# The off-diagonal parts of a block-diagonal product formed in one pass, and another order of the first loads, in a linear-attention and MLP kernel

## Chip, cores and metric

The kernel runs on one core of a Trainium2 chip. The metric is the device time of one execution in microseconds (us). Engines are named as in the profile: PE (TensorE, products), PEld (its weight loads), DVE (VectorE), ACT (ScalarE), POOL (GpSimd), SP (SyncE, which issues most DMAs). ACT has a DMA queue of its own. Each profiled span is shorter than the time of its execution, and not by the same amount everywhere: by 2.0 to 2.3 us in the kernels with the old overhang code, by about 1.7 us (1.7 to 2.0) in those with the new one.

## The reference, cut to what matters

```python
x = A_x                                  # [1, 2048, 640]
xn = _layernorm(x)
qkv = xn @ wqkv                          # 32 heads of 20 columns
pq, pk = phi(q), phi(k)                  # phi(t) = where(t > 0, t + 1, exp(t)) + 1e-6
kv  = einsum("bhsd,bhse->bhde", pk, v)   # one 20x20 matrix per head
num = einsum("bhqd,bhde->bhqe", pq, kv)
den = einsum("bhqd,bhd->bhq", pq, z) + 1e-6
out = x + (num / den) @ wo + mlp(xn)     # mlp: 640 -> 1536 -> 640, gelu
```

The kernel never forms v. It forms G = xnᵀ·pk and then kv = wvᵀ·G, masked to the heads, and KVW = kvᵀ·wo, so that attention ends in a single product with pq.

Of the kernel before, what the change touches and what calls it, by code (L numbers as in the profile page):

```python
# [9 lines left out]
ALU = mybir.AluOpType  # L10
BF16 = mybir.dt.bfloat16
# [4 lines left out]
def kernel(  # L16
# [12 lines left out]
    nc = tc.nc  # L29
    P = nc.NUM_PARTITIONS  # L30
# [3 lines left out]
    S, D = x2d.shape  # L34
    F = B_w1.shape[1]
    H = 32
    DH = D // H
    NT = S // P
    NC = D // P
    NJ = F // P  # L40
    TOK = 512
    NG = S // TOK
    TPG = TOK // P
    EPS = 1e-5
    HALF = D // 2
# [1 line left out]
    assert S % TOK == 0 and D % P == 0 and F % P == 0 and D == H * DH  # L47
    assert REST * TPG == TOK and NG * H == P

    e_lo = [m * P // DH * DH for m in range(NC)]  # L50
    e_rest = [min(H, (m * P + P - 1) // DH + 1) * DH - e_lo[m] - P for m in range(NC)]
    SKEW = DH - 4
    assert all(0 < r <= H for r in e_rest) and all(m * P - e_lo[m] <= SKEW for m in range(NC))

    ctx.enter_context(nc.allow_non_contiguous_dma(reason="small strided setup transfers"))

    consts = ctx.enter_context(tc.tile_pool(name="consts", bufs=1))
# [12 lines left out]
    GT = persist.tile([P, NC, D], BF16, name="GT")  # L70
    zacc = persist.tile([P, D], F32, name="zacc")
# [4 lines left out]
    wqk = early.tile([P, NC, 2 * D], BF16, name="wqk", tag="early")  # L76
    pk = mid.tile([P, NT, D], BF16, name="pk", tag="mid")

    wv = consts.tile([P, NC, D], BF16, name="wv")
    w1 = consts.tile([P, NC, F], BF16, name="w1")  # L80
    woA = consts.tile([P, NC, D], BF16, name="woA")
# [19 lines left out]
    def bank(dtype=F32, hold=False):  # L101
        n = turn.pop(0)
        if isinstance(hold, str):
            named[hold] = n
        else:
            (held if hold else turn).append(n)
        return psum.tile([P, TOK if dtype == F32 else 2 * TOK], dtype, name=f"bank{n}", tag=f"bank{n}")
# [16 lines left out]
    def load_x(t0, t1, queue=nc.sync):  # L124
        queue.dma_start(out=x_all[:, t0:t1, :], in_=xv[:, t0:t1, :])

    def load_wk(k0, k1):
        nc.scalar.dma_start(out=wqk[:, k0:k1, D : 2 * D], in_=wqkv_v[:, k0:k1, D : 2 * D])

    load_x(0, 1)  # L130
    load_x(1, 2, nc.scalar)
    load_x(2, 3)
    load_x(3, 4)

# [8 lines left out]

    nc.vector.memset(eps_t[:], EPS)
    nc.vector.memset(neg_half[:], -0.5)
    load_wk(0, 3)
    load_wk(3, NC)
    load_x(4, 8, nc.scalar)
# [13 lines left out]
            )  # L162

    WIDE = SKEW + P + H
    emask = consts.tile([P, NC + 2, WIDE], mybir.dt.int8, name="emask")
    emask_u = emask[:, :, SKEW : SKEW + P]

    def emask_parts():
        def select(block, q, base, sign, shift):
            nc.gpsimd.affine_select(  # L170
                out=emask[q, block, SKEW - shift : SKEW - shift + H // 4 * DH],
                in_=emask[q, block, SKEW - shift : SKEW - shift + H // 4 * DH],
                compare_op=ALU.is_ge, fill=0.0, base=base,
                pattern=[[-sign * DH, H // 4], [0, DH]], channel_multiplier=sign,
            )

        parts = [lambda: nc.gpsimd.memset(emask[:], 1.0)]
        for m in range(NC):
            i = m % NG
            for block, q, first in ((m, slice(0, P), 0), (NC + m // NG, slice(i * H, (i + 1) * H), P)):  # L180
                for base, sign in ((first, 1), (DH - 1 - first, -1)):
                    parts.append(
                        lambda block=block, q=q, base=base, sign=sign, m=m: select(block, q, base, sign, m * P - e_lo[m])
                    )
        return parts

    def emit_warm(n):
# [74 lines left out]
    def fill(it, n=None):  # L262
        for emit in it[:n]:
            emit()
        del it[:n]
# [94 lines left out]
    def gate(ap):  # L360
        nc.gpsimd.tensor_copy(out=gate_t[:], in_=ap)
# [93 lines left out]
    def emit_G_sums(*names):  # L455
        for name in names:
            out, a, b = {
                "S1": lambda: (g_S(1), g_S(2), g_left(0, 0)),
                "S2": lambda: (g_S(2), g_left(1, 1), g_S(3)),
                "S3": lambda: (g_S(3), g_left(0, 0), g_left(1, 0)),  # L460
                "S4": lambda: (g_S(4), g_left(0, 1), g_S(2)),
                "T1": lambda: (g_T(1), by_deep(g_right(0, 1)), by_deep(g_right(0, 0))),
                "T2": lambda: (g_T(2), by_deep(g_right(1, 1)), g_T(1)),
                "T3": lambda: (g_T(3), g_right(1, 1), g_right(0, 1)),
                "T4": lambda: (by_deep(g_T(4)), by_deep(g_right(1, 0)), g_T(2)),
            }[name]()
            nc.vector.tensor_tensor(out=out, in0=a, in1=b, op=ALU.add if name == "S1" else ALU.subtract)
# [274 lines left out]
    quads = [Quad(m) for m in range(NR)]  # L742
    q = quads[0]
# [21 lines left out]
    for q, last, (w, den) in zip(quads[1:], quads, work):  # L765
        q.P5()
        last.close("b" if last.m else "c")
        last.P7_odd()
        q.P6()
        fill(w, 0 if den else None)  # L770
        if last.m:
            last.close("c")
        last.close("f", gelu=False)
        fill(w)
        if q.m + 1 < NR and not den:
            quads[q.m + 1].P1()
        q.P7()
        last.gelu("f")
        if den:
            fill(den)  # L780
            quads[q.m + 1].P1()
    gate(hT[NG - 1][:, 2, 0:1])
    fill(emask_work)
    last = quads[-1]
# [95 lines left out]
    def scale(g, c, part=slice(0, TOK)):  # L880
        gs = slice(g * TOK + part.start, g * TOK + part.stop)
        nc.vector.tensor_tensor(out=pqT[:, c, gs], in0=pqT[:, c, gs], in1=xnT[:, c, gs], op=ALU.mult)  # L882
# [9 lines left out]
    load_rec(0)  # L892
    for m in range(NC):
        nc.sync.dma_start(out=woA[:, m, :], in_=A_wo[e_lo[m] : e_lo[m] + P, :])
    woB = zacc[:].bitcast(BF16).rearrange("p (a n) -> p a n", a=2)
    for m in range(NC):
        a, i = divmod(m, NG)
        r = e_rest[m]
        nc.sync.dma_start(
            out=woB[i * H : i * H + r, a, :], in_=A_wo[e_lo[m] + P : e_lo[m] + P + r, :]  # L900
        )
    emit_G_sums("T1", "T2", "T3", "S1")
    for t in (1, 1 + NH):
        emit_xb(t)
# [12 lines left out]
    first, second = (  # L917
        [lambda c=c, g=g, p=p: scale(g, c, p) for g in (2, 0) for c in range(NC)]
        for p in (slice(0, 2 * P), slice(2 * P, TOK))
    )  # L920
# [4 lines left out]
        both(lambda b: (b.product(name, p), b.done(name, k, r, c), fill(rest, ns[b.i])))  # L925

    late = mid.tile([P, NT, D], BF16, name="late", tag="mid")
    kv = late[:, 0:2, :].rearrange("p a n -> p (a n)")[:, 0 : (NC + 2) * P].rearrange("p (b n) -> p b n", n=P)
    KVW = late[:, 2 : 2 + NC, :]
    osbs = [late[:, 2 + NC + i, :] for i in range(6)]  # L930
    Tq = wv[:].rearrange("p c n -> p (c n)")[:, 0 : 4 * CH * HALF].bitcast(FP16).rearrange(
# [90 lines left out]
    kvps = [bank(), bank()]  # L1022
    for m in range(NC):
        a, i = divmod(m, NG)
        for j in range(NC):
            nc.tensor.matmul(
                kvps[a][:, i * P : (i + 1) * P], lhsT=wv[:, j, e_lo[m] : e_lo[m] + P],
                rhs=GT[:, j, m * P : (m + 1) * P], start=(j == 0), stop=(j == NC - 1),
            )
    for a in range(2):  # L1030
        ms = range(a * NG, min(NC, (a + 1) * NG))
        for j in range(NC):
            for m in ms:
                i = m % NG
                r = min(H, D - e_lo[m] - P)
                nc.tensor.matmul(
                    kvps[1][i * H : i * H + r, (a + 1) * P : (a + 2) * P],
                    lhsT=wv[:, j, e_lo[m] + P : e_lo[m] + P + r],
                    rhs=GT[:, j, m * P : (m + 1) * P], start=(j == 0), stop=(j == NC - 1),
                )  # L1040
    fill(rest)
    ps0 = kvps[0][:].rearrange("p (b n) -> p b n", n=P)
    ps1 = kvps[1][:].rearrange("p (b n) -> p b n", n=P)
    nc.vector.tensor_tensor(out=kv[:, 0:NG, :], in0=ps0, in1=emask_u[:, 0:NG, :], op=ALU.mult)
    nc.vector.tensor_tensor(
        out=kv[:, NG : NG + 2, :], in0=ps1[:, 0:2, :], in1=emask_u[:, NG : NG + 2, :], op=ALU.mult
    )
    r = e_rest[NC - 1]
    nc.vector.tensor_tensor(
        out=kv[0:r, NG + 2, :], in0=ps1[0:r, 2, :], in1=emask_u[0:r, NG + 2, :], op=ALU.mult  # L1050
    )

    def emit_KVW(ns):
        pss = [bank() for _ in range(NC)]
        for m, ps in enumerate(pss):
            nc.tensor.matmul(ps[:, 0:HALF], lhsT=kv[:, m, :], rhs=woA[:, m, ns], start=True, stop=False)
        for m, ps in enumerate(pss):
            a, i = divmod(m, NG)
            q = slice(i * H, i * H + e_rest[m])
            nc.tensor.matmul(  # L1060
                ps[:, 0:HALF], lhsT=kv[q, NC + a, :], rhs=woB[q, a, ns], start=False, stop=True
            )
        for m, ps in enumerate(pss):
            (nc.vector.tensor_copy if m % 2 and ns is halves[0] else nc.scalar.copy)(out=KVW[:, m, ns], in_=ps[:, 0:HALF])  # L1064

    p = pairs[0]
    p.open("b", hold=True)
    p.h("b", 2, True)
    emit_KVW(halves[0])
    fill(S_sums(0, q_of, Sq_of))  # L1070
    p.open("f", hold=True)
# [31 lines left out]
    for n, p in enumerate(pairs):  # L1103
        first, last = n == 0, n == NH - 1
        late = late_scales[: LATE[n]]
# [122 lines left out]
```

## The kernel before: the parts that the change touches

Loads at the start. `x_all` holds 16 tiles of 128 tokens (160 KB each). Tiles 0 to 3 are the first group, and are worked on one by one; tiles 4 to 7 come as one DMA with rows of 5 KB instead of 1.25 KB.

```python
load_x(0, 1)                    # SP queue
load_x(1, 2, nc.scalar)         # ACT queue
load_x(2, 3)                    # SP
load_x(3, 4)                    # SP
...
load_wk(0, 3)                   # K weights, ACT, 480 KB
load_wk(3, NC)                  # K weights, ACT, 320 KB
load_x(4, 8, nc.scalar)         # ACT, 640 KB
```

After this comes, for each tile: mean and variance on DVE (two halves), norm on DVE, transpose on PE, and the K product on PE. DVE takes these steps in program order (see the lines below), so it stops at the first tile that has not come.

kv near the end. D = 640 is five blocks of 128 columns, and a head has 20 columns, so each block of kv has an overhang of up to 32 rows beside its 128x128 diagonal part:

```python
for m in range(NC):                               # five diagonal blocks
    for j in range(NC):                           # 25 products 128x128x128
        nc.tensor.matmul(kvps[a][...], lhsT=wv[:, j, e_lo[m] : e_lo[m] + P], rhs=GT[:, j, m * P : (m + 1) * P], ...)
for a in range(2):                                # overhangs
    ...                                           # 25 products with 12 or 32 stationary columns
            nc.tensor.matmul(kvps[1][i * H : i * H + r, (a + 1) * P : (a + 2) * P],
                lhsT=wv[:, j, e_lo[m] + P : e_lo[m] + P + r], rhs=GT[:, j, m * P : (m + 1) * P], ...)
# DVE: three masked copies into kv; then for each half of the columns:
for m, ps in enumerate(pss):
    nc.tensor.matmul(ps[:, 0:HALF], lhsT=kv[:, m, :], rhs=woA[:, m, ns], start=True, stop=False)
for m, ps in enumerate(pss):                      # overhang, K = 12 to 32 rows, 128 columns
    nc.tensor.matmul(ps[:, 0:HALF], lhsT=kv[q, NC + a, :], rhs=woB[q, a, ns], start=False, stop=True)
```

## Time and profile before

| | before |
|---|---|
| median time | 197.51 us (6 runs, 197.21 to 199.71) |
| profiled execution | 200.89 us, span 198.7 us, mean granted clock 0.99 |
| PE in the chain that ended last | 93% |

The first lines are from the page of the kernel before: the span, PE's busy time, and the heads of the chain of waits followed back from the last instruction.

```profile
span 198.7 us, 3380 instructions
PE 191.3 (96%) x1260; PEld 112.3 (57%) x1260; DVE 163.3 (82%) x392; ACT 89.8 (45%) x165; POOL 21.1 (11%) x52
...
PE 93%; DMA 4%; DVE 1%; SPq 0%; issue 0%
```

PE bounds the kernel; apart from it only a wait for an x tile at the start shows. The next lines are the timeline of that start: start in us, duration in us, engine, line, operation, out<-in, count, and in brackets the idle time before it and what ended it.

```profile
0.80 0.39 ACTq L125 DMA_DIRECT2D x_all<-in_A_x_dram  x1
0.81 1.42 SPq L125 DMA_DIRECT2D x_all<-in_A_x_dram  x3
...
1.22 1.00 ACTq L128 DMA_DIRECT2D wqk<-in_A_wqkv_dram  x2
...
2.25 0.49 ACTq L125 DMA_DIRECT2D x_all<-in_A_x_dram  x1
...
4.04 0.89 DVE L201 BATCH_NORM_STATS2 stats<-x_all 128x6 f32<-128x320 bf16 x2 [3.07 <-DMA x_all<-in_A_x_dram]
...
9.75 0.49 DVE L201 BATCH_NORM_STATS2 stats<-x_all 128x6 f32<-128x320 bf16 x1 [1.75 <-DMA x_all<-in_A_x_dram]
10.16 0.43 DVE L221 TENSOR_SCALAR xn<-x_all,mv,rstd 128x640 bf16<-128x640 bf16 x1
...
10.65 0.71 PE L234 MATMUL bank_197<-identity,xn 128*128 128x128 bf16 x5 [1.86 <-DVE xn L221]
```

DVE waits for tile 0 until 4.04 us and for tile 3 until 9.75 us. The norm of tile 2 stands behind the statistics of tile 3 in program order, so it starts at 10.16 and PE at 10.65. This profile is of a slow run. Now the kv stage, same view and columns:

```profile
126.52 1.28 PE L1026 MATMUL bank_1440<-GT,wv 128*128 128x128 bf16 x20
...
127.64 0.44 PE L1026 MATMUL bank_1441<-GT,wv 128*128 128x128 bf16 x5
...
128.01 0.73 PE L1036 MATMUL bank_1441<-GT,wv 128*32 128x128 bf16 x25
...
128.67 0.99 PE L964 MATMUL bank_1498<-w_93,hT_79 128*128 128x320 bf16 x6
...
130.28 0.30 PE L1060 MATMUL bank_1508<-zacc,late 12*128 12x320 bf16 x1
130.42 0.29 PE L1060 MATMUL bank_1509<-zacc,late 12*128 12x320 bf16 x1
130.64 0.66 PEld L964 LDWEIGHTS <-xn 128*128 128x128 f16 x6 [0.26 <-issue]
130.65 0.99 PE L964 MATMUL bank_1529<-w_91,xn 128*128 128x320 f16 x6
```

L1036 is the 25 overhang products: 0.66 us from their start to that of the next product. L1060 is the overhang of KVW: its fifth product starts 0.14 us behind the fourth.

### The profile page before, as it was taken

The numbers are of one execution on the slowest core, as the hardware profiler recorded it, in microseconds if no ns is written. First come the engines' busy times: TensorE is split into PE (matmuls) and PEld (weight loads), VectorE is DVE, ScalarE is ACT, GpSimd is POOL, SyncE is SP. The second block draws the span as 40 slices with busy tenths as digits, with TensorE's granted clock in tenths as the row PEclk, the third lists the DMA queues.
The fourth block names the chain that finished last, engine by engine and source line by source line (L and its number), as shares of the span: only waits on it lengthen the run. The fifth ranks groups of instructions, "written<-read, shape, count | busy, mean of one in ns | idle before, by whom it ended". The sixth has DMA issues, their size and how long they took to land.

```text
span 198.7 us, 3380 instructions
## 1 busy us (share of the span) xinstructions
PE 191.3 (96%) x1260; PEld 112.3 (57%) x1260; DVE 163.3 (82%) x392; ACT 89.8 (45%) x165; POOL 21.1 (11%) x52
## 2 busy tenths in 40 slices
PE   7589999999999999999999999999999999999993
PEld 2255444544445454444444777757777777777772
DVE  1659896999699999879688889979999999786533
ACT  2427767457669768899786320050010010100100
POOL 1001244002308500000700000000000000000000
PEclk9969999999999999999999999999999999999999
DMA  5999524964134100000006975400200110110113
GB/s 199 335 290 380 183 61 107 311 223 93 39 132 106 30 0 2 0 0 3 0 0 145 335 235 164 139 0 2 69 0 0 69 66 13 55 69 0 66 35 101
DMA packets 24400, 20.15 MB, mean 101 GB/s; under 512 B 11120, under 2 KB 24000, under 8 KB 24384
## 3 DMA queue, kind: packets, MB, share of 16 engines
q1 hardware_dynamic: 23280, 18.13, 29.7%
q10 hardware_dynamic: 1104, 1.80, 2.5%
q8 instruction: 10, 0.16, 0.4%
q14 instruction: 6, 0.05, 0.1%
HBM read 12.72 MB, written 5.24 MB: 90 GB/s over the span
## 4 chain that ended last, share of the span: by engine, by line
PE 93%; DMA 4%; DVE 1%; SPq 0%; issue 0%
DMA x_all<-in_A_x_dram 4%; PE bank_1209 L795 2%; PE bank_1282 L824 2%; PE bank_1273 L824 2%; PE bank_2131 L964 1%; PE bank_2047 L964 1%; PE bank_1963 L964 1%; PE bank_1879 L964 1%; PE bank_1790 L964 1%; PE bank_1701 L964 1%; PE bank_1575 L964 1%; PE bank_1433 L964 1%; PE bank_1398 L824 1%; PE bank_1386 L824 1%; PE bank_205 L310 1%; PE bank_1529 L964 1%
## 5 line engine op out<-in xcount | busy, mean ns | idle before, releaser
L964 PEld LDWEIGHTS <-xn 128*128 128x128 f16 x198 | 19.0, 98 | 7.3 <-issue 0.3
L485 PEld LDWEIGHTS <-w_91 128*128 128x128 bf16 x120 | 11.7, 98 | 13.9
L201 DVE BATCH_NORM_STATS2 stats<-x_all 128x6 f32<-128x320 bf16 x32 | 13.7, 469 | 4.8 <-DMA x_all<-in_A_x_dram 4.8
L473 PEld LDWEIGHTS <-wqk 128*128 128x128 bf16 x100 | 9.6, 98 | 11.1
L310 PEld LDWEIGHTS <-xnT 128*128 128x128 bf16 x80 | 7.6, 103 | 7.2 <-issue 0.7
L824 PEld LDWEIGHTS <-xn 128*128 128x128 bf16 (+1 forms) x80 | 7.8, 98 | 3.0
L221 DVE TENSOR_SCALAR xn<-x_all,mv,rstd 128x640 bf16<-128x640 bf16 x16 | 6.2, 436 | 3.6 <-POOL rstd L217 3.6
L882 DVE TENSOR_TENSOR pqT<-pqT,xnT 128x256 bf16<-128x256 bf16 (+1 forms) x30 | 8.5, 326 | 0.0
L320 PEld LDWEIGHTS <-xnT 128*128 128x128 bf16 x80 | 6.0, 101 | 3.9 <-issue 0.6
L628 PEld LDWEIGHTS <-w_91 128*128 128x128 bf16 (+1 forms) x48 | 4.5, 98 | 5.8 <-issue 0.7
L979 PEld LDWEIGHTS <-Sq 128*128 128x128 f16 x66 | 6.4, 98 | 2.4
L170 POOL TENSOR_SCALAR_AFFINE_SELECT emask<-emask 128x160 int8<-128x160 int8 (+1 forms) x20 | 7.1, 362 | 1.2
L412 DVE TENSOR_TENSOR x_all<-x_all,b2b 128x640 bf16<-128x640 bf16 x16 | 7.0, 479 | 0.0
L271 DVE TENSOR_SCALAR pqT<-pqT 128x512 bf16<-128x512 bf16 x20 | 5.7, 284 | 0.7 <-ACT pqT L268 0.6
L979 PEld LDWEIGHTS <-pqT 128*128 128x128 bf16 x50 | 4.8, 98 | 1.9 <-issue 0.3
L964 PEld LDWEIGHTS <-hT_79 128*128 128x128 bf16 x48 | 4.6, 98 | 1.9
L964 PEld LDWEIGHTS <-hT_80 128*128 128x128 bf16 x48 | 4.7, 98 | 1.7
L1064 ACT CAST late<-bank_1505 128x320 bf16<-128x320 f32 x1 | 0.4, 426 | 10.9 <-PE bank_1509 L1060 10.9
L190 PE MATMUL bank_124<-const-bfloat16-1.0 128*128 128x512 bf16 x10 | 3.7, 546 | 0.8 <-PEq L1212 0.8
L873 DVE TENSOR_TENSOR Sq<-pqT 128x256 f16<-128x256 bf16 x16 | 4.3, 281 | 0.0
L727 DVE TENSOR_TENSOR pk<-pk,GT 128x512 bf16<-128x512 bf16 x10 | 4.2, 421 | 0.0
L628 PEld LDWEIGHTS <-wv 128*128 128x128 f16 x24 | 2.3, 98 | 3.0 <-issue 0.3
(645 smaller groups left out, 510.7 us busy)
## 6 DMA issues: line engine op xcount, KB each, us to landing
xnT<-rec_rows SPq DMA_DIRECT2D x20, 128.0 KB, 2.5
out_dram<-late SPq DMA_DIRECT2D x14, 160.0 KB, 1.9
w_91<-in_B_w_dram SPq DMA_DIRECT2D x2, 960.0 KB, 6.6
w_93<-in_B_w_dram SPq DMA_DIRECT2D x3, 640.0 KB, 7.6
x_all<-in_A_x_dram SPq DMA_DIRECT2D x2, 640.0 KB
wqk<-in_A_wqkv_dram SPq DMA_DIRECT2D x1, 800.0 KB, 7.9
wv<-in_A_wqkv_dram SPq DMA_DIRECT2D x1, 800.0 KB
woA<-in_A_wo_dram SPq DMA_DIRECT2D x5, 160.0 KB, 3.1
```

The source lines that it names most:

```text
L170: nc.gpsimd.affine_select(out=emask[q, block, SKEW - shift : SKEW - shift + H // 4 * DH], in_=emask[q, block, SKEW - shift : SKEW - shift ...
L201: nc.vector.bn_stats(out=st[:, half, :], in_=x_all[:, t, half * HALF : (half + 1) * HALF])
L221: nc.vector.tensor_scalar(out=xn[:, t, ds], in0=x_all[:, t, ds], scalar1=mv[:, t, 0:1], scalar2=rstd[:, t : t + 1], op0=ALU.subtract, op1= ...
L310: nc.tensor.matmul(K_ps[t][:], lhsT=xnT[:, k, t * P : (t + 1) * P], rhs=wqk[:, k, D : D + TOK], start=(k == 0), stop=(k == NC - 1),)
L412: nc.vector.tensor_tensor(out=x_all[:, t, :], in0=x_all[:, t, :], in1=b2b[:], op=ALU.add)
L473: nc.tensor.matmul(ps[:], lhsT=wqk[:, k, m * P : (m + 1) * P], rhs=xnT[:, k, gs], start=(k == 0), stop=(k == NC - 1),)
L485: nc.tensor.matmul(ps[:], lhsT=w1[:, k, j * P : (j + 1) * P], rhs=xnT[:, k, g * TOK : (g + 1) * TOK], start=(k == 0), stop=(k == NC - 1),)
L628: nc.tensor.matmul(self.ps[name][:], lhsT=left[:, c, js], rhs=x_block(*block, c) if block else Tx({4: 3, 5: 0, 6: 1, 7: 2}[p], c), start=( ...
L824: nc.tensor.matmul(ps if len(right.shape) == 3 else ps.rearrange("p (c n) -> p c n", c=NC), lhsT=left[:, t, self.i], rhs=right[:, t], star ...
L882: nc.vector.tensor_tensor(out=pqT[:, c, gs], in0=pqT[:, c, gs], in1=xnT[:, c, gs], op=ALU.mult)
L964: nc.tensor.matmul(self.ps[name][:, cols], lhsT=left[:, j], rhs=right[:, j, cols], start=(start and j == 0), stop=False, skip_group_check= ...
L979: nc.tensor.matmul(self.ps[name][:, cols], lhsT=left[:, c], rhs=right[:, c, cols], start=False, stop=(stop and c == CH - 1), skip_group_ch ...
```

## The change

It has three parts. The overhangs: instead of 25 products, five of full size give four windows of 32x32, which cover four of the overhangs (the last block is moved so that it ends with the matrix, which makes its overhang an 8-column piece of the fourth). The loads: x tile 1 goes to SP, and the K weights wait for a memset on their target. The order: the product P1 of the next MLP step is put ahead of the attention denominators. Cut to its core:

```diff
-    load_x(1, 2, nc.scalar)
+    load_x(1, 2)
...
+    nc.vector.memset(wqk[:, 0, D : D + TOK], 0.0)
     load_wk(0, 3)
...
         if den:
+            quads[q.m + 1].P1()
             fill(den)
-            quads[q.m + 1].P1()
...
+    nc.gpsimd.tensor_copy(out=wvw..., in_=wv[:, :, P : P + NG * WE]...[:, :, :, 0:H])   # the four windows' columns
...
-    for a in range(2):           # 25 products on strips
-        ...
+    wins = kvps[1][:, P : 2 * P].rearrange("p (i n) -> p i n", i=NG)
+    for j in range(NC):
+        nc.tensor.matmul(wins, lhsT=wvw[:, j], rhs=GT[:, j, P - H + 8 : ...][:, :, 0:H], start=(j == 0), stop=(j == NC - 1))
...
-            nc.tensor.matmul(ps[:, 0:HALF], lhsT=kv[q, NC + a, :], rhs=woB[q, a, ns], start=False, stop=True)
+            nc.tensor.matmul(ps[rows, 0:HALF], lhsT=kvw[q, i, cols], rhs=woB[q, ns], start=False, stop=True, ...)
```

Here `rows` and `cols` pick a 32x32 square (8 columns for the fifth), so that a product uses 32 rows and 32 columns of the PE array.

More of the change, by code (lines that the diff above doesn't have):

```diff
@@ L48 @@
     assert REST * TPG == TOK and NG * H == P
-    e_lo = [m * P // DH * DH for m in range(NC)]
-    e_rest = [min(H, (m * P + P - 1) // DH + 1) * DH - e_lo[m] - P for m in range(NC)]
+    e_lo = [m * P // DH * DH for m in range(NC - 1)] + [D - P]
+    WQ, WE = P - 24, P - 8
     SKEW = DH - 4
-    assert all(0 < r <= H for r in e_rest) and all(m * P - e_lo[m] <= SKEW for m in range(NC))
+    assert DH == 20 and NC == 5 and all(m * P % DH <= SKEW for m in range(NC))
     ctx.enter_context(nc.allow_non_contiguous_dma(reason="small strided setup transfers"))
@@ L164, with select, heads @@
     WIDE = SKEW + P + H
-    emask = consts.tile([P, NC + 2, WIDE], mybir.dt.int8, name="emask")
+    emask = consts.tile([P, NC + 1, WIDE], mybir.dt.int8, name="emask")
     emask_u = emask[:, :, SKEW : SKEW + P]
     def emask_parts():
-        def select(block, q, base, sign, shift):
+        def select(out, base, sign, pattern):
             nc.gpsimd.affine_select(
-                out=emask[q, block, SKEW - shift : SKEW - shift + H // 4 * DH],
-                in_=emask[q, block, SKEW - shift : SKEW - shift + H // 4 * DH],
-                compare_op=ALU.is_ge, fill=0.0, base=base,
-                pattern=[[-sign * DH, H // 4], [0, DH]], channel_multiplier=sign,
+                out=out, in_=out, compare_op=ALU.is_ge, fill=0.0, base=base, pattern=pattern, channel_multiplier=sign
+            )
+        def heads(block, q, e0, q0, sign):
+            start = q0 - q0 % DH
+            select(
+                emask[q, block, SKEW - q0 % DH :][:, 0 : H // 4 * DH], e0 - start if sign > 0 else start + DH - 1 - e0,
+                sign, [[-sign * DH, H // 4], [0, DH]],
             )
         parts = [lambda: nc.gpsimd.memset(emask[:], 1.0)]
-        for m in range(NC):
-            i = m % NG
-            for block, q, first in ((m, slice(0, P), 0), (NC + m // NG, slice(i * H, (i + 1) * H), P)):
-                for base, sign in ((first, 1), (DH - 1 - first, -1)):
-                    parts.append(
-                        lambda block=block, q=q, base=base, sign=sign, m=m: select(block, q, base, sign, m * P - e_lo[m])
-                    )
+        areas = [(m, slice(0, P), e_lo[m], m * P) for m in range(NC)]
+        areas += [(NC, slice(i * H, (i + 1) * H), P + i * WE, WQ + i * P) for i in range(NG)]
+        for area in areas:
+            for sign in (1, -1):
+                parts.append(lambda area=area, sign=sign: heads(*area, sign))
+        w3 = emask[3 * H :, NC, SKEW:]
+        e3 = P + 3 * WE
+        parts.append(lambda: select(w3[:, 0 : P - WQ], e3 - e_lo[3] - P, 1, [[0, P - WQ]]))
+        parts.append(lambda: select(w3[:, P - WQ : H], e_lo[4] - 1 - e3, -1, [[0, H - (P - WQ)]]))
         return parts
@@ L894 @@
         nc.sync.dma_start(out=woA[:, m, :], in_=A_wo[e_lo[m] : e_lo[m] + P, :])
-    woB = zacc[:].bitcast(BF16).rearrange("p (a n) -> p a n", a=2)
-    for m in range(NC):
-        a, i = divmod(m, NG)
-        r = e_rest[m]
-        nc.sync.dma_start(
-            out=woB[i * H : i * H + r, a, :], in_=A_wo[e_lo[m] + P : e_lo[m] + P + r, :]
-        )
+    woB = zacc[:].bitcast(BF16)[:, 0:D]
+    for i in range(NG):
+        nc.sync.dma_start(out=woB[i * H : (i + 1) * H, :], in_=A_wo[P + i * WE : P + i * WE + H, :])
+    wvw = zacc[:].bitcast(BF16)[:, D : 2 * D].rearrange("p (c n) -> p c n", c=NC)
+    nc.gpsimd.tensor_copy(
+        out=wvw.rearrange("p c (i n) -> p c i n", i=NG),
+        in_=wv[:, :, P : P + NG * WE].rearrange("p c (i n) -> p c i n", i=NG)[:, :, :, 0:H],
+    )
     emit_G_sums("T1", "T2", "T3", "S1")
@@ L927 @@
     late = mid.tile([P, NT, D], BF16, name="late", tag="mid")
-    kv = late[:, 0:2, :].rearrange("p a n -> p (a n)")[:, 0 : (NC + 2) * P].rearrange("p (b n) -> p b n", n=P)
+    kv = late[:, 0, :].rearrange("p (b n) -> p b n", n=P)
+    kvw = late[:, 1, 0 : NG * (H + 8)].rearrange("p (i n) -> p i n", i=NG)
+    nc.gpsimd.memset(kvw[:, :, 0:8], 0.0)
     KVW = late[:, 2 : 2 + NC, :]
@@ L1029 @@
             )
-    for a in range(2):
-        ms = range(a * NG, min(NC, (a + 1) * NG))
-        for j in range(NC):
-            for m in ms:
-                i = m % NG
-                r = min(H, D - e_lo[m] - P)
-                nc.tensor.matmul(
-                    kvps[1][i * H : i * H + r, (a + 1) * P : (a + 2) * P],
-                    lhsT=wv[:, j, e_lo[m] + P : e_lo[m] + P + r],
-                    rhs=GT[:, j, m * P : (m + 1) * P], start=(j == 0), stop=(j == NC - 1),
-                )
+    wins = kvps[1][:, P : 2 * P].rearrange("p (i n) -> p i n", i=NG)
+    for j in range(NC):
+        nc.tensor.matmul(
+            wins, lhsT=wvw[:, j],
+            rhs=GT[:, j, P - H + 8 : P - H + 8 + NG * P].rearrange("p (i n) -> p i n", i=NG)[:, :, 0:H],
+            start=(j == 0), stop=(j == NC - 1),
+        )
     fill(rest)
     ps0 = kvps[0][:].rearrange("p (b n) -> p b n", n=P)
-    ps1 = kvps[1][:].rearrange("p (b n) -> p b n", n=P)
     nc.vector.tensor_tensor(out=kv[:, 0:NG, :], in0=ps0, in1=emask_u[:, 0:NG, :], op=ALU.mult)
+    nc.vector.tensor_tensor(out=kv[:, NG, :], in0=kvps[1][:, 0:P], in1=emask_u[:, NG, :], op=ALU.mult)
     nc.vector.tensor_tensor(
-        out=kv[:, NG : NG + 2, :], in0=ps1[:, 0:2, :], in1=emask_u[:, NG : NG + 2, :], op=ALU.mult
-    )
-    r = e_rest[NC - 1]
-    nc.vector.tensor_tensor(
-        out=kv[0:r, NG + 2, :], in0=ps1[0:r, 2, :], in1=emask_u[0:r, NG + 2, :], op=ALU.mult
+        out=kvw[:, :, 8:], in0=wins, in1=emask_u[:, NC, 0:H].unsqueeze(1).to_broadcast((P, NG, H)), op=ALU.mult
     )
@@ L1055, in emit_KVW @@
         for m, ps in enumerate(pss):
-            nc.tensor.matmul(ps[:, 0:HALF], lhsT=kv[:, m, :], rhs=woA[:, m, ns], start=True, stop=False)
+            nc.tensor.matmul(ps[:, 0:HALF], lhsT=kv[:, m, :], rhs=woA[:, m, ns], start=True, stop=True)
         for m, ps in enumerate(pss):
-            a, i = divmod(m, NG)
-            q = slice(i * H, i * H + e_rest[m])
+            i, rows, cols = (m, slice(P - H, P), slice(0, H)) if m < NG else (NG - 1, slice(0, 8), slice(H, H + 8))
+            q = slice(i * H, (i + 1) * H)
             nc.tensor.matmul(
-                ps[:, 0:HALF], lhsT=kv[q, NC + a, :], rhs=woB[q, a, ns], start=False, stop=True
+                ps[rows, 0:HALF], lhsT=kvw[q, i, cols], rhs=woB[q, ns], start=False, stop=True, skip_group_check=True
             )
```

## The prediction

> **What bounds the kernel now.** TensorE. In the chain of work that ended last, PE is 93% of the 198.7 us span. From 10.65 us on the chain stays on PE; before that it is one DMA (x_all, 4%) and VectorE. The profiled run was slow (200.89 us against a median of 197.51).
>
> **The start.** In the timeline VectorE's first statistics wait for x tile 0 until 4.04 us; then VectorE is nearly gapless (stats 0.9, center 0.4, stats 0.9 ...) until it waits for x tile 3, which landed at 9.75 us. That holds norm(2) until 10.16 and PE until 10.65, and the granted clock falls to 0.5 until 13.6 us. About 2 us of wait and 1.5 us of clock: just the 3.4 us by which this run is slow. The DMA packets show x tile 3 done by about 6.5 us on nearly all engines; on one its rows alternated with the 5 KB rows of tiles 4 to 7 until 9.2. I take it that the fast runs don't have this wait and are bound by tile 0's landing and VectorE. The Trainium skill ("DMA: Bandwidth & Descriptors", "Queues, rings and completion order") says each DMA engine round-robins between the queue rows; the alternating packets agree.
>
> The change sends tile 0 first and alone: tile 1 moves behind it on SP, and the K weights wait for a VectorE memset (estimate 0.2 to 0.3 us, from the 0.28 us of a 128x512 bf16 tensor_scalar). Both tiles' packets now share 1.9 to 3.5 us, so tile 0 should land 0.3 to 0.5 us earlier, and PE's start with it: **-0.4 us**. Against it: x tile 3 is now the fourth issue on SP, nearer to x tiles 4 to 7, and may land later (needed by about 7.7 us).
>
> **P1 before the denominators.** PE waits about 0.15 us for Z3t (0.32 us on VectorE) before the 20 den products at 95.01. P1 (0.43) fits there: **-0.1 us**.
>
> **kv.** The 25 strip products take 128.01 to 128.67: 26 ns each, 0.66 us, plus a gap of about 0.08. Five 128x128x128 products at 56 ns (as the 20 before them) are 0.28: **-0.4 us**. VectorE's masking stays about equal (0.68+0.42+0.27 against 0.68 and two of 0.27). It starts at 128.19 because VectorE is busy until then; the first K=128 product of KVW needs the 128x512 part, about 128.9, and PE will be there at about 129.1. So the saving is just not swallowed.
>
> **KVW rests.** From 130.18 to 130.65 per half: four K=12..32 products start together at 130.28, the fifth 0.14 later. With 32x32 squares the four still overlap; the fifth shares their row group but not their columns, so it may overlap: 0 to -0.14 per half, **-0.1 us** in all.
>
> Off the path: the POOL copy of wv's columns (estimate 1 to 1.5 us near 116).
>
> Sum: about -1.1 us. **Predicted 196.4 us, range 195.4 to 197.6.** Faster by over 2%: 0.05; within 2%: 0.93; slower: 0.02.
>
> **What would show it.** First statistics at about 3.6 us; kv plus rests on PE about 1.4 us, not 1.98; no wait between P7 and den; KVW's first product with no wait for the mask.
>
> **What would make it wrong.** x tile 3 later or earlier than I think: if the fast runs did have the 9.75 us wait and the new order cures it, -3 us; if tile 3 slips past 8 us, +1 to +3. POOL's copy slowing VectorE before 128 us.

## The result

| | before | after |
|---|---|---|
| median | 197.40 us (20 runs, 197.01 to 199.71) | 197.26 us (10 runs, 196.95 to 197.46) |
| ratio of fast runs | | 0.998, 95% interval 0.9958 to 1.0002 |
| profiled | 198.7 us span (slow) | 195.3 us span (fast) |

A ratio here is the mean time of one kernel's fast runs over that of the other's in the same rounds, so it is not quite the ratio of the medians that are quoted. The verdict is "same": a gain of 0.4 us by the ratio, of 0.14 by the medians, and none is inside the interval, where 1.1 us were forecast. The time lies in the forecast range, the gain does not come near its forecast size.

The start after the change, same view as before:

```profile
0.81 1.82 SPq L125 DMA_DIRECT2D x_all<-in_A_x_dram  x4
...
0.99 0.27 DVE L146 MEMSET wqk<- 128x256 uint32 x1
...
1.29 0.96 ACTq L128 DMA_DIRECT2D wqk<-in_A_wqkv_dram  x2
...
2.28 0.49 ACTq L125 DMA_DIRECT2D x_all<-in_A_x_dram  x1
...
3.06 0.89 DVE L209 BATCH_NORM_STATS2 stats<-x_all 128x6 f32<-128x320 bf16 x2 [1.80 <-DMA x_all<-in_A_x_dram]
...
6.13 0.89 DVE L209 BATCH_NORM_STATS2 stats<-x_all 128x6 f32<-128x320 bf16 x2 [0.46 <-DMA x_all<-in_A_x_dram]
...
8.66 0.49 DVE L209 BATCH_NORM_STATS2 stats<-x_all 128x6 f32<-128x320 bf16 x1 [1.09 <-DMA x_all<-in_A_x_dram]
9.07 0.43 DVE L229 TENSOR_SCALAR xn<-x_all,mv,rstd 128x640 bf16<-128x640 bf16 x1
...
13.12 1.24 PE L318 MATMUL bank_255<-wqk,xnT 128*128 128x512 bf16 x5
```

Tile 0 comes 1 us earlier (3.06). But DVE now waits 0.46 us for tile 2 and 1.09 us for tile 3, and the norm of tile 2 starts at 9.07. The last line is the last K product of the first group; the chain of waits has been on PE since 9.55 us. Against the kernel before, the gate moves next to nothing: the K weights are issued at 1.29 instead of 1.22, because before the change the ACT queue was busy with x tile 1 until then. But with tile 1 off that queue they would go out at 0.80 without a gate, and that is worse (`no_gate` below).

The kv stage after the change:

```profile
123.72 1.28 PE L1037 MATMUL bank_1442<-GT,wv 128*128 128x128 bf16 x20
...
125.12 0.44 PE L1043 MATMUL bank_1443<-GT,zacc 128*128 128x128 bf16 x5
...
125.40 0.98 PE L975 MATMUL bank_1480<-w_93,hT_79 128*128 128x320 bf16 x6
...
127.00 0.30 PE L1063 MATMUL bank_1490<-zacc,late 32*32 32x320 bf16 x1
127.00 0.29 PE L1063 MATMUL bank_1491<-zacc,late 32*8 32x320 bf16 x1
127.23 0.66 PEld L975 LDWEIGHTS <-xn 128*128 128x128 f16 x6
127.23 0.99 PE L975 MATMUL bank_1511<-w_91,xn 128*128 128x320 f16 x6
```

From the start of the diagonal products to the next MLP product it is now 125.40 - 123.72 = 1.68 us (2.15 before), and the fifth overhang product of KVW starts with the fourth. So the kv part did what was hoped, and more.

### The profile page after: what moved, and what is told of

Read it like the earlier page. It is cut to its first block, busy times and chain, and to the rows that moved or that the text cites. A ratio compares the mean times of both kernels' runs of the same rounds, so it can differ in the third digit from the quotient of the medians.

```text
span 195.3 us, 3345 instructions
## 1 busy us (share of the span) xinstructions
PE 189.1 (97%) x1240; PEld 111.4 (57%) x1240; DVE 163.7 (84%) x393; ACT 89.8 (46%) x165; POOL 22.3 (11%) x54
## 4 chain that ended last, share of the span: by engine, by line
PE 93%; DMA 3%; DVE 1%; SPq 1%; issue 0%
DMA x_all<-in_A_x_dram 3%; PE bank_1210 L803 2%; PE bank_1283 L832 2%; PE bank_1274 L832 2%; PE bank_2113 L975 1%; PE bank_2029 L975 1%; PE bank_1945 L975 1%; PE bank_1861 L975 1%; PE bank_1772 L975 1%; PE bank_1683 L975 1%; PE bank_1557 L975 1%; PE bank_1435 L975 1%; PE bank_1399 L832 1%; PE bank_1387 L832 1%; PE bank_1511 L975 1%; PE bank_2042 L975 1%
## 5 line engine op out<-in xcount | busy, mean ns | idle before, releaser
L318 PEld LDWEIGHTS <-xnT 128*128 128x128 bf16 x80 | 7.3, 98 | 7.5 <-issue 0.9
L328 PEld LDWEIGHTS <-xnT 128*128 128x128 bf16 x80 | 5.8, 98 | 3.5
L172 POOL TENSOR_SCALAR_AFFINE_SELECT emask<-emask 128x160 int8<-128x160 int8 (+3 forms) x20 | 6.7, 347 | 0.9
```

What stands on the lines that cost most here:

```text
L172: nc.gpsimd.affine_select(out=out, in_=out, compare_op=ALU.is_ge, fill=0.0, base=base, pattern=pattern, channel_multiplier=sign)
L318: nc.tensor.matmul(K_ps[t][:], lhsT=xnT[:, k, t * P : (t + 1) * P], rhs=wqk[:, k, D : D + TOK], start=(k == 0), stop=(k == NC - 1),)
```

## Experiments

**A fast profile of the kernel before.** The first profile was slow, so it could not be set against the one after. The unchanged kernel was profiled again.

> The kernel before, unchanged, for a profile in the fast state (the one at hand is slow by 3.4 us). Theory A (the new load order delays x tile 3 and eats what kv gains): a fast run has no wait for x tile 3, or a short one; tile 3 is usable by about 8.2 us; PE's last K tile starts near 12.5 us (13.28 after the change); and from there to the end it takes 182.7 us as in the slow profile (182.0 after the change). Theory B (the start is as good as before or better, and the kv part saved nothing in the fast state): the last K tile starts at 13.3 us or later and the rest takes about 182.0 us. Theory C: the slow state is not the start at all; then the start looks as in the slow profile, with tile 3 at 9.75 us and the clock at 0.5.

It came out at 197.42 us, span 195.2 us, clock 1.0. The timeline of its start:

```profile
4.04 0.89 DVE L201 BATCH_NORM_STATS2 stats<-x_all 128x6 f32<-128x320 bf16 x2 [3.07 <-DMA x_all<-in_A_x_dram]
...
7.90 0.49 DVE L201 BATCH_NORM_STATS2 stats<-x_all 128x6 f32<-128x320 bf16 x1
...
8.30 0.43 DVE L221 TENSOR_SCALAR xn<-x_all,mv,rstd 128x640 bf16<-128x640 bf16 x1
...
12.35 1.24 PE L310 MATMUL bank<-wqk,xnT 128*128 128x512 bf16 x5
```

After tile 0 nothing is waited for. The norm of tile 2 starts at 8.30 us, against 9.07 after the change (+0.77), and the last K product at 12.35 against 13.12 (+0.77). Theory A stands: the start has become 0.77 us slower. The extra time of the slow profile is the wait for tile 3 (norm of tile 2 at 10.16 instead of 8.30) and the lower clock behind it (a mean of 0.57 from 10 to 14 us, and 1.0 here), since the two profiles differ in nothing else of that size. Other slow runs were not profiled. That the wait brought the clock down is not shown: in the profile of `no_gate` below PE waits longer (2.25 us, until 9.74), and the clock stays at 1.0.

**The two halves of the change alone.** `loads_only` is the kernel before with the two load edits; `rest_only` is the change without them.

```diff
 loads_only, on the kernel before:
-    load_x(1, 2, nc.scalar)
+    load_x(1, 2)
+    nc.vector.memset(wqk[:, 0, D : D + TOK], 0.0)
 rest_only, on the changed kernel: the same three lines the other way round
```

> Before, with the change's load order alone (x tile 1 on SP, memset ahead of the K weights). Theory A: 0.5 to 0.9 us slower than before; tile 3 statistics again start near 8.7 us with a wait of about 1 us on the DMA. Theory B: same as before or up to 0.4 us faster. My prediction said 0.4 us faster.

> The change without its load order (x tile 1 back on the ACT queue, no memset); kv, KVW and P1 parts kept. Theory A: 0.5 to 0.8 us faster than before, so about 196.7 us. Theory B: no faster than 0.2 us. The prediction's sum for these parts was 0.6.

`loads_only`: 198.50 us median, ratio to before 1.0053 (1.0036 to 1.0070), so about 1.0 us slower. `rest_only`: 196.40 us, ratio 0.9953 (0.9933 to 0.9973), so about 0.9 us faster. The two nearly cancel, as the result says. The rival, that kv saved nothing, falls. The start of `loads_only`, and then PE's last product in the fast profiles of the kernel before, the change, `rest_only` and `loads_only`, in this order:

```profile
6.33 0.89 DVE L202 BATCH_NORM_STATS2 stats<-x_all 128x6 f32<-128x320 bf16 x2 [0.63 <-DMA x_all<-in_A_x_dram]
...
8.44 0.49 DVE L202 BATCH_NORM_STATS2 stats<-x_all 128x6 f32<-128x320 bf16 x1 [0.67 <-DMA x_all<-in_A_x_dram]
...
12.90 1.24 PE L311 MATMUL bank<-wqk,xnT 128*128 128x512 bf16 x5
```

```profile
191.91 0.22 PE L986 MATMUL bank<-late,pqT 128*128 128x128 bf16 x1
191.84 0.22 PE L997 MATMUL bank_2134<-late,pqT 128*128 128x128 bf16 x1
191.04 0.22 PE L996 MATMUL bank<-late,pqT 128*128 128x128 bf16 x1
192.46 0.22 PE L987 MATMUL bank<-late,pqT 128*128 128x128 bf16 x1
```

In `loads_only` tiles 2 and 3 are waited for as after the change, tile 3 for less than the 1 us expected, and the last K product starts 0.55 us late (12.90 against 12.35). PE ends 0.87 us earlier in `rest_only`, in line with its time, and 0.55 us later in `loads_only`: the rest of its 1.0 us lies behind PE's last product or outside the span, and is not explained.

**What delays tiles 2 and 3.** `x4_sp` takes x tiles 4 to 7 from the ACT queue and puts them behind tile 3 on SP.

```diff
     load_x(3, 4)
+    load_x(4, 8)
...
-    load_x(4, 8, nc.scalar)
```

> The whole change, with x tiles 4 to 7 moved from the ACT queue to the SP queue, behind x tile 3, so that tile 3 shares the DMA engines with the K weights alone. Theory A: tile 3 lands by about 7.5 us, no wait for it, PE's last K tile starts about 1.2 us earlier than after the change (near 12 us), and the time is 0.8 to 1.3 us below the change, near 196.2. Rival A2 (it is the later K weights, which made PE wait until 6.29 us for its first K product, not tile 3): less than 0.3 us gained, since the K weights come no earlier here.

196.03 us median, ratio 0.9932 (0.9913 to 0.9951): the fastest of all, 0.7% below before. Theory A's time came out, but not by its path, and rival A2 falls on the time. The profiled run (196.65 us, the slowest of its six) shows:

```profile
6.92 0.89 DVE L209 BATCH_NORM_STATS2 stats<-x_all 128x6 f32<-128x320 bf16 x2 [1.13 <-DMA x_all<-in_A_x_dram]
...
8.05 0.59 PE L318 MATMUL bank<-wqk,xnT 128*128 128x512 bf16 x2 [0.83 <-DMA wqk<-in_A_wqkv_dram]
```

Tile 3 isn't waited for any more; tile 2 and the second K weights are. The last K product starts at 12.73 us, 0.4 us earlier than after the change, and this run is 0.4 us faster than the profiled run of the change. What the faster runs of this kernel look like was not profiled.

**How long the K weights are held back.** Three kernels differ from the change in one line each: no memset at all, one of 888 words, one of 1280.

```diff
 no_gate:    -    nc.vector.memset(wqk[:, 0, D : D + TOK], 0.0)
 gate_mid:   -    nc.vector.memset(wqk[:, 0, D : D + TOK], 0.0)
             +    nc.vector.memset(wqk[:, 0:3, D : D + TOK + 80], 0.0)
 gate_long:  -    nc.vector.memset(wqk[:, 0, D : D + TOK], 0.0)
             +    nc.vector.memset(wqk[:, 0:4, D : D + TOK + P], 0.0)
```

> The whole change without its memset; x tile 1 stays on SP, so the K weights are the first issue of the ACT queue at 0.80 us. Theory F: the first K weights (480 KB) go ahead of x tile 1, whose statistics wait beyond 5 us; x tiles 2 and 3 come later still, behind x tiles 4 to 7; time 0.5 to 2 us above the change. Rival R: within 0.3 us of the change, since 0.3 us of gate more or less does little.

> The whole change with a longer memset ahead of the K weights (888 instead of 256 words a partition, estimate 0.93 us from the 0.27 us of the change's), so that they are issued near 1.95 us: after x tile 2 (1.7) and before x tile 3 (2.2). Theory F (the data moves about in the order in which the two queues issue, so it matters before which x tile the K weights are issued): tile 2 follows tile 1 at once and lands by 4.8 us; no wait for it; tile 3 still comes late, usable near 7 us; norm of tile 2 near 7.6 to 8.3 us; time 0.5 to 1.2 us below the change. Rival R (the queues share the DMA engines row by row from the start, so a gate only shifts the K weights by its own length): tile 2 gains at most 0.3 us, tile 3 is still waited for past 8.3 us, time within 0.3 us of the change.

> The whole change with a memset of 1280 words (estimate 1.33 us), so that the K weights are issued near 2.36 us, after all four x tiles. Theory F: tiles 0 to 3 land one after the other, tile 3 by about 5 us; VectorE never waits for a tile after tile 0; the K weights land near 6 and 7 us, so that the first K products wait instead; norm of tile 2 near 7.6 us, last K tile near 11.9 us (13.28 after the change), time 0.8 to 1.4 us below the change, near 196.1. Rival R: as for the mid gate, within 0.3 us of the change.

On where the tiles go, theory F was right. These are KB moved by the two queues in half microseconds, added up from the DMA packets of the traces by the time at which each ended (SP / ACT; up to 7.5 us SP carries x tiles 0 to 3, without tile 1 in the kernel before):

| us | before, fast | after | gate_long |
|---|---|---|---|
| 2.0 to 3.0 | 82 / 105 | 203 / 0 | 264 / 0 |
| 3.0 to 4.0 | 123 / 214 | 109 / 123 | 241 / 0 |
| 4.0 to 4.5 | 89 / 105 | 1 / 179 | 54 / 14 |
| 4.5 to 5.5 | 54 / 328 | 152 / 224 | 75 / 243 |
| 5.5 to 6.5 | 127 / 224 | 80 / 287 | 0 / 344 |
| 6.5 to 7.5 | 6 / 390 | 72 / 308 | 0 / 346 |

After the change tile 2, third on SP (its issue starts near 1.7 us), has to let the first K weights (issued at 1.29) go ahead: from 4.0 to 4.5 us SP moves 1 KB. Tile 3 then meets tiles 4 to 7. With the long gate all four tiles are through by about 5 us. In these traces the order of issue over both queues decides about when a DMA starts to move. It does not decide the shares from then on: there the rows of the two queues take turns, which favours the 5 KB rows of tiles 4 to 7.

The medians were `gate_mid` 198.68 us (ratio 1.0056), `gate_long` 198.13 (1.0022), `no_gate` 198.06 (1.0060). For `no_gate` this is what F expected, 0.8 us above the change; for the two gates it is not. Their runs fall into two kinds. Of the long gate's six, two took 196.55 and 196.71 us at clock 1.0 (0.6 us below the change), three 198.5 to 198.9 at 0.988 to 0.990, and one 197.74 at 1.0. Of the mid gate's six, one took 196.77 and one 198.04 us at 1.0, and four 198.3 to 199.7 at 0.989 or 0.990. All of them count as fast. The quick ones come near F: in the profile of `gate_mid` (196.77 us) tile 2 is not waited for and its norm starts at 8.12, but PE waits 1.00 and 0.42 us for K weights. The profile of a quick run of `gate_long` shows what is waited for there:

```profile
2.36 0.97 ACTq L128 DMA_DIRECT2D wqk<-in_A_wqkv_dram  x2
...
7.16 1.44 PE L318 MATMUL bank<-wqk,xnT 128*128 128x512 bf16 x5 [1.55 <-DMA wqk<-in_A_wqkv_dram]
7.36 0.43 DVE L229 TENSOR_SCALAR xn<-x_all,mv,rstd 128x640 bf16<-128x640 bf16 x1
```

The norm of tile 2 starts at 7.36 us, 1.7 us earlier than after the change, but PE waits 1.55 us for K weights. The wait has been turned round, not taken away. Without a gate, it is tile 2 that comes late:

```profile
8.24 0.89 DVE L208 BATCH_NORM_STATS2 stats<-x_all 128x6 f32<-128x320 bf16 x2 [1.59 <-DMA x_all<-in_A_x_dram]
```

Its issue starts at 1.72 us, just before that of tiles 4 to 7 (1.83), but from 6.0 to 7.5 us the packets of the two queues take turns: 79 rows of 1.25 KB start, and 96 rows of 5 KB.

**Is it PE's idle stretch that splits the runs?** `gate_long_warm` fills it.

```diff
-    emit_warm(1)
+    emit_warm(7)
```

> The long gate, with six more idle warm-up products (0.2 us each) on PE before the first K product, where PE stood idle from 5.6 to 7.16 us. In four of six runs of the long gate the mean granted clock was 0.99 or the time 1 to 2 us longer. Theory H: PE's idle stretch let the clock fall in those runs; with the gap filled all runs come out near 196.5 with the clock at 1.0. Rival: the spread has another cause (the DMA order itself), and stays at 196.5 to 199.

All six runs came within 196.76 to 197.48 us, at clocks of 0.997 to 1.0 (ratio 0.9966, 0.9936 to 0.9996). The slow kind of run is gone, as theory H says; the level is 0.5 us above the 196.5 expected, and this ran on another chip than the long gate.

**Tiles 4 to 7 behind tile 3 in the other orders.** The edit of `x4_sp`, made on `no_gate` and on `rest_only`.

> The whole change, no memset, x tiles 4 to 7 on SP behind tile 3. Theory F: the ACT queue holds the K weights alone and the four tiles come in between; tile 2, which was waited for until 8.24 us without the gate because tiles 4 to 7 were issued before it (1.83 us on ACT), is usable by about 6.6 us, and the time falls from 198.06 to about 196.0 to 196.6. Rival (K weights ahead of tile 1 are the harm): stays above 197.3.

> The kernel parts of the change with the old load order, and x tiles 4 to 7 on SP behind tile 3. In the fast state tile 3 was not waited for in the old order (used at 7.90 us, landed near 6.7), so moving tiles 4 to 7 behind it should gain nothing: same as rest_only, 196.2 to 196.6. If it is over 0.4 us faster, something else than the wait for tile 3 is bought by that move.

`no_gate_x4sp`: 196.64 us, with all six runs inside 0.12 us, ratio 0.9941 (0.9916 to 0.9967). Tile 2 is used at 6.89 us, near the 6.6 expected (though tiles 4 to 7 were not issued before it, as the expectation has it, but 0.1 us behind). On this chip before itself spread from 197.11 to 199.91 (median 198.14), so the ratio is rough. `rest_x4sp` missed its expectation: its four fast runs took 196.94, 197.11, 197.16 and 199.57 us (ratio 0.9995, 0.9943 to 1.0047), two more were slow (200.30 and 200.75), and even the quick ones are above the 196.2 to 196.6 expected. Its profile (197.11 us) shows PE waiting for the second K weights:

```profile
8.54 0.59 PE L317 MATMUL bank<-wqk,xnT 128*128 128x512 bf16 x2 [1.32 <-DMA wqk<-in_A_wqkv_dram]
```

In the old order tiles 4 to 7 had stood behind those weights on the ACT queue, and now rows of both take turns in the packets. Moving them is no gain as such.

**Tiles 4 to 7 out of the way of both.** They are issued once tile 1's statistics are done, held back by a memset of one column.

```diff
-    load_x(4, 8, nc.scalar)
...
+        nc.vector.memset(x_all[:, TPG, 0:1], 0.0)
+        load_x(4, 8)
         nc.vector.memset(w1[:, 0, 0:1], 0.0)
```

> The whole change, with x tiles 4 to 7 taken off both queues until x tile 1's statistics are done (a one-column memset ahead of them, issue near 5.7 us on SP, in front of w1), so that neither x tile 3 nor the second K weights share the DMA engines with them. Theory A: the wait for tile 3 (1.09 us, until 8.66) vanishes or falls under 0.3 us, without a new one for the K weights; norm of tile 2 by about 8.2 us instead of 9.07; time 0.7 to 1.2 us below the change, so about 1.3 to 1.8 us (0.7 to 0.9%) below before. Rival: tile 3 is late because it is issued behind the K weights, not because of tiles 4 to 7; then less than 0.4 us below the change.

> The kernel parts of the change with the old load order, x tiles 4 to 7 late in the same way. Nothing waited for tiles or K weights in fast runs of this order, so the fast runs should equal rest_only (about 0.5% below before); but fewer runs with a granted clock of 0.99 and 2 to 3 us more. If it is more than 0.4 us better than that, the old order too lost time to tiles 4 to 7.

The start did what theory A said, and the time did not: `after_xlate` 197.38 us, ratio 0.9986 (0.9965 to 1.0006); `rest_xlate` 197.16, ratio 0.9984 (0.9964 to 1.0004). The timeline of `after_xlate`:

```profile
6.04 0.89 DVE L210 BATCH_NORM_STATS2 stats<-x_all 128x6 f32<-128x320 bf16 x2 [0.28 <-DMA x_all<-in_A_x_dram]
...
7.81 0.43 DVE L230 TENSOR_SCALAR xn<-x_all,mv,rstd 128x640 bf16<-128x640 bf16 x1
...
11.86 1.24 PE L319 MATMUL bank<-wqk,xnT 128*128 128x512 bf16 x5
...
34.06 0.39 PE L319 MATMUL bank<-wqk,xnT 128*128 128x512 bf16 x1 [1.23 <-DMA xnT<-xn_rows]
```

There is no wait for tile 3, and the last K product starts at 11.86 us instead of 13.12. So tile 3 was late because of tiles 4 to 7, and not just because it is issued behind the K weights: here it still is. But the second group (tiles 4 to 7) is now later by itself, and PE waits 1.23 us for its transposed rows at 34 us. What was won by 11.86 us is lost there: behind that wait PE runs 0.4 us later than in the changed kernel, and so to the end. `rest_xlate` missed its expectation (0.5% below before) in the same place: the first K product of its second group takes PE from 32.13 to 34.02 us, with waits for the transposed rows, against 32.01 to 33.09 in `rest_only`.

## Why the prediction was wrong

- **The start, "-0.4 us": this is the step that failed.** It measured +0.77 us on the critical path in the profile of the change (norm of tile 2 from 8.30 to 9.07) and +0.55 us in that of `loads_only`, whose time rose by about 1.0 us. Its first half was right and even too small: tile 0 lands 1 us earlier, not 0.3 to 0.5. What it added up wrongly is the rest: "PE's start with it" takes for granted that nothing behind tile 0 is waited for. The prediction named the danger (tile 3 needed by 7.7 us, and "if tile 3 slips past 8 us, +1 to +3") but gave it no share of the sum; tile 3 was usable at 8.66. Tile 2's wait (0.46 us) it did not see at all.
- **Why it mis-sized it.** It argued from round-robin sharing between the two queues. The Trainium skill ("DMA: Bandwidth & Descriptors", "Queues, rings and completion order") says that each DMA engine takes turns between the queue rows it has work for. On a single engine the trace agrees: in the slow profile the last rows of tile 3 alternate one by one with 5 KB rows of tiles 4 to 7, 0.25 us a pair. But when a DMA starts to move follows the issue order over both queues (table above), and the order of issue is what the change altered: tile 2 had to let the first K weights go ahead. Tile 3's wait, in contrast, is due to tiles 4 to 7, and goes when they are out of the way (`after_xlate`).
- "I take it that the fast runs don't have this wait": the second profile has none, and its span is 3.5 us shorter.
- **P1 before the denominators, "-0.1 us".** From the start of the sum product (L369, L377) to that of the first product behind both P1 and the denominators: 2.39 us before (94.26 to 96.65), 2.28 after (91.56 to 93.84). It measured 0.11. (This and the two parts below are read from the slow profile of the kernel before; the fast one gives the same differences.)
- **kv, "-0.4 us".** It measured 0.47 (2.15 to 1.68); 0.38 is the products themselves (0.66 to 0.28), the rest the gap before them. The "26 ns each" is a mean: the 25 products took ten steps of about 56 ns, and now it is five.
- **KVW rests, "-0.1 us".** The two halves went from 1.98 and 1.97 us (128.67, 130.65, 132.62) to 1.83 and 1.85 (125.40, 127.23, 129.08): 0.27. The chance taken half was won whole: the fifth product overlaps. The Trainium skill ("TensorE: Matmul & The Clock Gate", "Part 3: Packing small matmuls — row/col tiling") says that products in different tiles of the array run concurrently; the trace agrees, with the two last starting at 127.00 though they share their row group.
- **The sum.** The parts behind the start gave 0.11 + 0.47 + 0.27 = 0.85 us, not 0.6, in line with `rest_only` (0.47% of 197.4 is 0.93; PE's end 0.87 earlier). The start took 0.77 of it back. What is left is 0.08 us in the profiles, and PE's last product does start 0.07 us earlier. Between the two profiled runs, the rest of the gain in time (197.42 to 197.04) lies outside the spans (195.2 and 195.3 us), and no run shows what it is.
- **"The saving is just not swallowed" by DVE's masking** held: after the change the masked copy of 128x512 starts at 125.39 and the first KVW product at 126.22, right behind the MLP product. POOL's copy of the windows took 1.63 us at 110.9, far from anything that waits.

What stays open: the slower kind of run of the two gates, 1.5 to 3 us above the quick ones, goes with a clock of 0.99 and, for the long gate, is gone when PE's idle stretch is filled. But none of these runs was profiled, the filled version ran on another chip, and the quick profiles have the same stretch at full clock, so the link is supported and not shown. Which waits the faster runs of `x4_sp` have is not known either. The better versions all keep the kernel parts: with the old loads (`rest_only`, ratio 0.9953) and with tiles 4 to 7 behind tile 3 (`x4_sp`, 0.9932, and on another chip `no_gate_x4sp`, 0.9941). The intervals of the first two overlap at 0.993 to 0.995, and the same move of tiles 4 to 7 did badly in the old order on another chip, so what is safe to conclude is to keep the kernel parts and drop the change's load order.

## What to carry to other kernels

A start that loads several inputs at once has a due date for each, and taking one forward puts another back: list the due dates of all (here tile 0, tile 2, the K weights, tile 3, and the second group near 33 us) before moving one, and look in the order of issue for what will stand before it. Judge a gate by what it moves the issue past: here it kept the K weights near their old place (1.29 us, not 0.80, which cost 0.8 us), and a gate until 2.36 us put them behind all four tiles, so that PE waited for them instead. And when two edits go in together, time them apart; 0.9 us of gain was hidden behind 1.0 us of loss.

## What the Trainium skill lacked or had wrong

- "DMA: Bandwidth & Descriptors": it describes turns between queues on one engine, but not when a DMA gets its first turn if another queue has issued before. After the change x tile 2 was issued near 1.7 us and SP moved 1 KB from 4.0 to 4.5 us, while the K weights, issued 0.4 us earlier on ACT, moved 179 KB. With the long gate the K weights were issued at 2.36 us and their first row started at 3.97, when about four fifths of SP's tiles had moved.
- The same page gives about 0.6 us to the first byte for DMAs from SP and ACT. It does not say from where this is counted. After the change the first row of tile 0 starts at 1.82 us: 1.0 us from the start of its issue (0.81), and the 0.6 us from the end of it (1.20).
- The same page has an engine drain a packet of about 9 to 17 descriptors before it switches queues. In the slow profile one row of tile 3 (1.25 KB) and one of tiles 4 to 7 (5 KB) take turns, so that the queue with short rows gets a fifth of the bytes.
- "TensorE: Matmul & The Clock Gate" asks for no PE gap above about 3 us. In the slow profile PE's gap was 1.86 us (8.8 to 10.65), amid a thinly used stretch, and the mean clock from 10 to 14 us was 0.57. In the profile of `no_gate` a gap of 2.25 us left it at 1.0, so the length of the gap alone does not decide.
- The same page says that the time from start to start never drops below about 25 ns. That does not hold for products on different columns of the array: four strip products start within 11 ns, some 2 to 4 ns apart, and only the next four start 56 ns later.
